# The second stage in two passes, with its weights prepared while the first stage still runs

## The chip, the cores and the metric

The kernel runs on one core of a Trainium2 chip. The metric is the device time of one execution in microseconds (us). The engines are TensorE (PE: matrix multiplies; PEld: its weight loads), VectorE (DVE), ScalarE (ACT), GpSimd (POOL) and SyncE (SP), which issues the DMAs. Each engine takes its instructions in a fixed order that is set when the kernel is built.

## The reference

Three blocks follow one another. The inputs are `q`, `k`, `v` of 8 batches, 8 heads, 576 positions and 64 columns, `phi` with 32 memory slots, and weights.

```python
# 1: attention over 32 memory slots, for each batch and head
a = softmax(phi, axis=positions)               # 576 x 32
k_m, v_m = a.T @ k, a.T @ v                    # 32 x 64
attn = softmax(q @ k_m.T / 8)                  # 576 x 32
x = attn @ v_m                                 # all heads side by side: 4608 x 512
# 2: gated layer, d_ff = 1536
x = (silu(x @ w_gate) * (x @ w_val)) @ w_out   # 4608 x 512
# 3: second layer, d_ff = 2048
h = x @ w_in
x = where(h > 0, h, exp(min(h, 0)) - 1) @ w_out2
```

The weights arrive as 64-bit floats, everything else in 32 bits.

## The kernel before

**Precision.** Each operand is split into a high part and a low part, and every product is made as three matmuls (high by high, low by high, high by low). A weight tile of 128 x 512 is loaded raw (64-bit, 512 KB) into a buffer `wr` and split by `split_w` (lines 71 to 85): two ScalarE copies (L77, L83), four VectorE instructions (L78, L79, L81, L82) that use a scratch tile `wc`, and two GpSimd instructions (L84, L85). L84 and L85 make the low part. `load_w` (L92) does this for one tile and takes two tiles from a pool, `whi` and `wlo`. There are 68 such loads: 24 of `w1g` (gate and value, in six pairs `p` of units with four pieces each), 12 of `w1o` (the output weight of each of 12 units) and 32 of `w2` (for the last block).

**Stage one** (the loop over batches `b`, L407) works on units 0 to 3 of the 12 units of the gated layer. `vw` (L112) multiplies the small matrix v_m by the gate and value weights of a pair, so that `gate1` and `val1` can multiply the attention weights `at` by the result directly. `down1` multiplies by the output weight and stores a partial sum to DRAM (`p1_d`, copied by L402). Beside it, a list `todo` of small tasks is worked off by `tick()`, a few after each unit: the back half of the attention of batch b+1 (q, scores, softmax, the transposed result `at`, stored at L340) and the front half of batch b+2 (phi, k, v; it ends in the store of `vt` at L280). All attention tiles lie in one pool, `at`. When batch 6 has been issued, this pool is closed, the pool `wb` of 32 weight tiles takes its room, and the loads of `w1g` pairs 2 to 4 and of four output weights are issued; the rest of the stage-two weights goes to pool `wa` (24 tiles), whose tiles held the weights of stage one.

**Stage two** (L512) goes once over all batches, two halves of 288 positions each. It reads `at` and `vt` back from DRAM, works on units 4 to 11, and sums their outputs in four PSUM accumulators `acc0` to `acc3`. `down2` lags two units behind. After unit 11, four VectorE additions (L486) add the partial sum, read from DRAM into the single buffer `p1`, and the result goes to `x1_d`. One unit is 12 matmuls for gate and value and 12 for the output, 288 columns wide; the `vw` of the next batch add 48 matmuls of 512 columns per batch.

**Stage three** (L594) takes nine blocks of 512 rows through 16 units with `w2`; all its matmuls are 512 columns wide. Twenty of the 32 loads of `w2` are written in stage two, twelve after it.

**Order.** The build places instructions by a simulated timeline. An instruction that comes later in the code may go ahead of others on its engine when its operands and its buffers are free.

Of the kernel before, what the change touches and what calls it, by code (L numbers as in the profile page):

```python
# [21 lines left out]
KD = DM // 128  # L22
# [7 lines left out]
NWB = 32  # L30
NWC = 8
# [3 lines left out]
def attention_moe_moe(ctx: ExitStack, tc: tile.TileContext, qT, phiT, kv, w1g, w1o, w2, out):  # L35
# [9 lines left out]
    wr_p = ctx.enter_context(tc.tile_pool(name="wr", bufs=2))  # L45
    wt_p = ctx.enter_context(tc.tile_pool(name="wt", bufs=1))
# [14 lines left out]
    ps_at = st_ps.enter_context(tc.tile_pool(name="ps_at", bufs=2, space=PSUM))  # L61
    st_at = ExitStack()
    at_p = st_at.enter_context(tc.tile_pool(name="at", bufs=1))
# [3 lines left out]
    p1_d = [dram.tile([128, KD, S], F32, name=f"p1d{b}") for b in range(B)]  # L67
    x1_d = [dram.tile([128, KD, S], F32, name=f"x1d{b}") for b in range(B)]


    def split_w(raw, hi, lo):
        lo32, hi32 = raw[:, :, 0], raw[:, :, 1]
        v = wt_p.tile([128, 512], F32, tag="wv", name="wv", bufs=2)
        c = wt_p.tile([128, 512], I32, tag="wc", name="wc")
        vi, cf = v.bitcast(I32), c.bitcast(F32)

        act(out=v, in_=hi32.bitcast(F32), func=AF.Copy, scale=2.0 ** -112)  # L77
        nc.vector.tensor_scalar(out=c, in0=vi, scalar1=3, scalar2=None, op0=ALU.logical_shift_left)  # L78
        stt(out=vi, in0=vi, scalar=-2 ** 31, in1=c, op0=ALU.bitwise_and, op1=ALU.bitwise_or)  # L79

        nc.vector.tensor_scalar(out=c, in0=vi, scalar1=-2 ** 23, scalar2=None, op0=ALU.bitwise_and)  # L81
        stt(out=cf, in0=lo32.bitcast(U32), scalar=2.0 ** -52, in1=cf, op0=ALU.mult, op1=ALU.mult)  # L82
        act(out=hi, in_=v, func=AF.Copy)  # L83
        nc.gpsimd.tensor_tensor(out=v, in0=v, in1=hi.bitcast(F32), op=ALU.subtract)  # L84
        nc.gpsimd.tensor_tensor(out=lo, in0=v, in1=cf, op=ALU.add)  # L85
# [77 lines left out]
    ident = at_p.tile([128, 128], F32, tag="ident", name="ident")  # L163
    make_identity(nc, ident)
    mask = at_p.tile([128, 4, 64], F32, tag="mask", name="mask")
# [14 lines left out]
    class Batch:  # L180
# [4 lines left out]
        def load_phi(self):  # L185
            self.ph = at_p.tile([128, 2, S], F32, tag="ph", name="ph")
            nc.sync.dma_start(out=self.ph, in_=phiT[self.b].rearrange("g p s -> p g s"))

        def load_kv(self, c):
            n = chunk(c)  # L190
            t = at_p.tile([128, 2, 512], F32, tag="kvr", name="kvr", bufs=2)
            nc.sync.dma_start(out=t[:n], in_=kv[self.b, 128 * c:128 * c + n])
            self.kvr[c] = t

        def load_q(self, c):
            n = chunk(c)
            t = at_p.tile([128, 512], F32, tag="qr", name="qr", bufs=2)
            nc.sync.dma_start(out=t[:, :4 * n], in_=qT[self.b, :, 512 * c:512 * c + 4 * n])
            self.qr[c] = t


        def phi(self):
            ph = self.ph
            nmx = at_p.tile([128, 2], F32, tag="nmx", name="nmx")
            nc.vector.tensor_reduce(out=nmx, in_=ph, op=ALU.max, axis=AX.X, negate=True)
            sm = at_p.tile([128, 2], F32, tag="sm", name="sm")
            for g in range(2):
                act(out=ph[:, g, :], in_=ph[:, g, :], func=AF.Exp, bias=nmx[:, g:g + 1],
                    accum_out=sm[:, g:g + 1])
            self.rs = at_p.tile([128, 2], F32, tag="rs", name="rs", bufs=2)  # L210
            nc.vector.tensor_scalar_add(out=self.rs, in0=sm, scalar1=1e-9)
            nc.vector.reciprocal(out=self.rs, in_=self.rs)

        def a_T(self, c0):
            if c0 == 0:
                self.ah = at_p.tile([128, NCH, 256], F32R, tag="ah", name="ah")
                self.al = at_p.tile([128, NCH, 256], F32R, tag="al", name="al")
# [12 lines left out]
        def kv_prep(self, c):  # L230
            n = chunk(c)
            t = self.kvr.pop(c)
            hi = at_p.tile([128, 2, 512], F32R, tag="kvh", name="kvh", bufs=2)
            lo = at_p.tile([128, 2, 512], F32R, tag="kvl", name="kvl", bufs=2)
            act(out=hi[:n], in_=t[:n], func=AF.Copy)
            lo_part(self.b and LO_KV[c], lo[:n], t[:n], hi[:n])
            self.kvs[c] = hi, lo
# [14 lines left out]
        def kv_out(self):  # L252
            self.kvm = at_p.tile([128, 2, 2, 256], F32, tag="kvm", name="kvm")
            mk = mask.rearrange("p h d -> p (h d)").unsqueeze(1).to_broadcast([128, 2, 256])
            for g in range(2):
                stt(out=self.kvm[:, g], in0=self.kvp[g], scalar=self.rs[:, g:g + 1], in1=mk,
                    op0=ALU.mult, op1=ALU.mult)

        def k_T(self):
# [4 lines left out]
            self.kT = at_p.tile([128, 2, 2, 128], F32R, tag="kT", name="kT")  # L264
# [17 lines left out]
        def q_prep(self, c):  # L282
            n = 4 * chunk(c)
            t = self.qr.pop(c)
            hi = at_p.tile([128, 512], F32R, tag="qh", name="qh", bufs=2)
            lo = at_p.tile([128, 512], F32R, tag="ql", name="ql", bufs=2)
# [4 lines left out]
        def score(self, c):  # L291
            n = chunk(c)
            if c == 0:
                self.sc = at_p.tile([128, NCH, 256], F32, tag="sc", name="sc")
# [6 lines left out]
            t = at_p.tile([128, 4, 64], F32, tag="sct", name="sct", bufs=2)  # L301
# [8 lines left out]
        def soft(self, c0, c1):  # L310
            n, k, sc = self.rows(c0, c1)
            mx = at_p.tile([128, 32, 1], F32, tag="mx", name="mx")[:n, :k]
# [4 lines left out]
        def soft2(self, c0, c1):  # L317
            n, k, sc = self.rows(c0, c1)
            sm = at_p.tile([128, 32, 1], F32, tag="smx", name="smx")[:n, :k]
# [85 lines left out]
    wl = []  # L405
    for b in range(B):
        todo = []  # L407
        bk = list(back_tasks(b + 1)) if b + 1 < B else []
        fr = list(front_tasks(b + 2)) if b + 2 < B else []
        for i in range(max(len(bk), len(fr))):  # L410
            todo += fr[i:i + 1] + bk[i:i + 1]
        if b + 1 < B:
            todo += vw_tasks(b + 1)
        done = [0, 0]

        def tick():
            done[0] += 1
            upto = min(len(todo), -(-len(todo) * (done[0] + 3) // 12))
# [17 lines left out]
        if b == B - 2:  # L436
            st_at.close()
            st_ps.close()
            wb_p = ctx.enter_context(tc.tile_pool(name="wb", bufs=NWB))
            for p in range(2, 5):  # L440
                for k in range(KD):
                    load_wg(p, k, wb_p)
                if p < 4:
                    for u in (2 * p, 2 * p + 1):
                        load_wo(u, wb_p)


    ps_acc = ctx.enter_context(tc.tile_pool(name="ps_acc", bufs=1, space=PSUM))
    ps_vw = ctx.enter_context(tc.tile_pool(name="ps_vw", bufs=1, space=PSUM))
    st_p1 = ExitStack()  # L450
    p1_p = st_p1.enter_context(tc.tile_pool(name="p1", bufs=1, side="right"))
    load_wo(8, wa_p)
    load_wo(9, wa_p)
    for k in range(KD):
        load_wg(5, k, wa_p)
    load_wo(10, wa_p)
    load_wo(11, wa_p)
# [3 lines left out]
    def more_w2(pool, n):  # L461
# [3 lines left out]
    at2, vt2 = {}, {}  # L465

    def load2(b):
        vt2[b] = av_p.tile([128, 2, KD, 128], F32R, tag="vt", name="vt2")
        nc.sync.dma_start(out=vt2[b].bitcast(F32), in_=vt_d[b].bitcast(F32))
        at2[b] = av_p.tile([128, 2, 2, S], F32R, tag="at", name="at2")  # L470
        nc.sync.dma_start(out=at2[b].bitcast(F32), in_=at_d[b].bitcast(F32))

    def load_p1(b, hf):
        t = p1_p.tile([128, KD, HS], F32, tag="p1", name="p1l")
        nc.sync.dma_start(out=t, in_=p1_d[b][:, :, HS * hf:HS * hf + HS])
        return t

    def down2(q):
        b, hf, u, hs, accs, p1 = q
        if u == UA:  # L480
            accs += [ps_acc.tile([128, HS], F32, tag=f"acc{m}", name=f"acc{m}") for m in range(KD)]
        for m in range(KD):
            down(accs[m], WO[u][0], hs, slice(128 * m, 128 * m + 128), u == UA, u == NU1 - 1)
        if u == NU1 - 1:
            for m in range(KD):
                tt(out=p1[:, m, :], in0=accs[m], in1=p1[:, m, :], op=ALU.add)  # L486
            nc.sync.dma_start(out=x1_d[b][:, :, HS * hf:HS * hf + HS], in_=p1)
# [17 lines left out]

    LAG = 2
    pend = []
    load2(0)
    for p in range(UA // 2, NU1 // 2):
        vw(0, p, vt2[0], ps_vw, "vw")  # L510
    vwq = []
    for b in range(B):  # L512
        for hf in range(2):
            p1 = load_p1(b, hf)
            accs = []
            if hf == 0 and b + 1 < B:
                load2(b + 1)
            for u in range(UA, NU1):
                s = gate1(b, u, at2[b], HS * hf)
                pend.append((b, hf, u, val1(b, u, at2[b], HS * hf, s), accs, p1))  # L520
                if len(pend) > LAG:
                    down2(pend.pop(0))
                if vwq:
                    q = vwq.pop(0)
                    vw(q[0], q[1], vt2[q[0]], ps_vw, "vw", (q[2],))
                    if q[0] == B - 1 and q[2] == 1:
                        more_w2(wb_p if q[1] < 5 else wa_p, 4)
                if hf == 1 and u % 2 == 1:
                    if b + 1 < B:
                        vwq += [(b + 1, u // 2, 0), (b + 1, u // 2, 1)]  # L530
                    elif u // 2 == 3:
                        nxt = load3(0)
                if b == 2 and hf == 0 and u % 2:
                    more_w2(wa_p, 1)
    for q in pend:
        down2(q)
    pend = []
    st_p1.close()
    st_r.close()
    more_w2(wb_p, 4)  # L540
    more_w2(wa_p, 4)
    wc_p = ctx.enter_context(tc.tile_pool(name="wc", bufs=NWC))
    more_w2(wc_p, 4)
# [93 lines left out]
```

## Time and profile before

| | |
|---|---|
| median of 3 runs | 1789.2 us (1788.12 to 1793.85) |
| the profiled execution | 1791.92 us, span 1790.1 us |
| mean granted TensorE clock | 0.971 of full speed |
| TensorE busy | 1708.9 us (95%) |
| VectorE busy | 1047.8 us (59%) |
| ScalarE busy | 770.8 us (43%) |
| GpSimd busy | 277.6 us (16%) |
| moved by DMA | 144.68 MB |

Busy times are sums over the whole span and hide the stages: stage one runs until some 470 us, stage two to 1000, stage three to the end. Matmuls overlap, so a busy TensorE is not one at its peak; counts of matmuls per us are a sharper measure. A row of the timeline names the line, the operation and, in brackets, how long the engine was idle before it and what ended the wait. In the stretches, PEclk is the granted clock as a share of full speed.

### The profile page before, as it was taken

The page shows a single profiled execution, that of the slowest core. Times are in us where ns is not written, and L with a number is a line of the kernel's source. Part 1 is how long each engine was busy: PE and PEld are TensorE (multiplying, and loading weights), DVE is VectorE, ACT ScalarE, POOL GpSimd, SP SyncE. Part 2 cuts the span into 40 slices and gives each one's busy share as a digit, 9 for nine tenths or more (in the row PEclk, how much of TensorE's full clock was granted, in tenths as well). Part 3 has the DMA queues.
Part 4 walks back from the last instruction along what each step waited for, and adds up shares of the span by engine and source line. Part 5 has one row for each costly group of instructions (what it writes and reads, how often), then busy time and mean ns, then how long its engine had stood idle before and what let it go on. Part 6 is the DMA issues. An engine that isn't in the chain of part 4 may idle for free.

```text
span 1790.1 us, 24102 instructions
## 1 busy us (share of the span) xinstructions
PE 1708.9 (95%) x9424; PEld 1496.5 (84%) x9424; DVE 1047.8 (59%) x1781; ACT 770.8 (43%) x1447; POOL 277.6 (16%) x197
## 2 busy tenths in 40 slices
PE   6689999999869999999999999999999999999998
PEld 4478998898759999999999878888888888888887
DVE  6887677657665333333368887455545555555554
ACT  5567666654433222322345444343434343434332
POOL 3552222114442000000034441000000000000000
PEclk8779999999969999999999999999999999999999
DMA  6555444234434121112225221010101010101000
GB/s 217 181 183 192 155 158 155 65 116 148 139 104 166 54 66 66 67 52 79 67 75 169 92 83 48 1 48 0 48 1 48 1 48 1 47 1 47 1 24 24
DMA packets 68209, 144.68 MB, mean 81 GB/s; under 512 B 7168, under 2 KB 38912, under 8 KB 66048
## 3 DMA queue, kind: packets, MB, share of 16 engines
q1 hardware_dynamic: 68096, 143.16, 24.1%
q8 instruction: 73, 1.20, 0.3%
q14 instruction: 40, 0.33, 0.1%
HBM read 101.19 MB, written 41.94 MB: 80 GB/s over the span
## 4 chain that ended last, share of the span: by engine, by line
PE 78%; DVE 9%; DMA 4%; ACT 3%; issue 2%; POOL 2%; SPq 0%; ACTq 0%; POOLq 0%; DVEq 0%
PE acc L581 7%; PE acc L582 7%; PE acc L583 7%; PE pu L557 7%; PE pu L555 6%; PE pu L556 6%; PE acc L139 3%; PE acc L138 3%; PE acc L137 3%; PE pg L132 2%; PE pv L132 2%; PE pg L133 2%; PE pg L134 2%; PE pv L134 2%; PE pv L133 2%
## 5 line engine op out<-in xcount | busy, mean ns | idle before, releaser
L581 PE MATMUL acc<-whi,hh 128*128 128x512 f32 x576 | 224.8, 390 | 3.3 <-ACT hh L143 3.3
L555 PE MATMUL pu<-x1s,whi 128*128 128x512 f32 x576 | 224.2, 389 | 1.6 <-DVE g L571 1.6
L582 PE MATMUL acc<-wlo,hh 128*128 128x512 f32 x576 | 224.2, 389 | 0.0
L557 PE MATMUL pu<-x1s,wlo 128*128 128x512 f32 x576 | 224.1, 389 | 0.0
L556 PE MATMUL pu<-x1s,whi 128*128 128x512 f32 x576 | 224.1, 389 | 0.0
L583 PE MATMUL acc<-whi,hl 128*128 128x512 f32 x576 | 223.0, 390 | 0.0
L570 DVE SCALAR_TENSOR_TENSOR g<-e,g 128x512 f32<-128x512 f32 x144 | 104.8, 727 | 157.1 <-ACT g L569 156.9
L84 POOL TENSOR_TENSOR wv<-wv,whi 128x512 f32<-128x512 f32 x68 | 102.1, 1501 | 587.3 <-ACT whi L83 469.6
L143 ACT ACTIVATE hh<-g 128x512 fp32r<-128x512 f32 x144 | 90.9, 632 | 217.0 <-DVE g L571 212.4
L159 DVE TENSOR_TENSOR h<-s,pv 128x288 f32<-128x288 f32 x192 | 86.5, 451 | 164.5 <-PE pv L134 135.3
L568 ACT ACTIVATE e<-g 128x512 f32<-128x512 f32 x144 | 90.8, 631 | 205.5 <-DVE g L567 205.2
L138 PE MATMUL acc<-hh,wlo 128*128 128x288 f32 x512 | 151.7, 298 | 2.7 <-POOL wlo L85 2.7
L145 DVE TENSOR_TENSOR hl<-g,hh 128x512 fp32r<-128x512 f32 x144 | 100.3, 697 | 87.0 <-ACT hh L143 87.0
L139 PE MATMUL acc<-hl,whi 128*128 128x288 f32 x512 | 149.7, 298 | 0.7 <-DVE hl L145 0.7
L137 PE MATMUL acc<-hh,whi 128*128 128x288 f32 x512 | 150.1, 296 | 0.3 <-ACT hh L143 0.3
L145 DVE TENSOR_TENSOR hl<-h,hh 128x288 fp32r<-128x288 f32 x192 | 108.4, 565 | 61.7 <-ACT hh L143 61.2
L143 ACT ACTIVATE hh<-h 128x288 fp32r<-128x288 f32 x192 | 85.0, 443 | 124.4 <-DVE h L159 123.9
L152 ACT ACTIVATE s<-pg 128x288 f32<-128x288 f32 x192 | 78.1, 408 | 123.6 <-PE pg L134 122.6
L581 PEld LDWEIGHTS acc<-whi,hh 128*128 128x128 f32 x576 | 108.1, 188 | 27.8 <-ACT hh L143 5.7
L567 DVE TENSOR_SCALAR g<-pu 128x512 f32<-128x512 f32 x144 | 99.3, 689 | 53.5 <-PE pu L557 53.3
L555 PEld LDWEIGHTS pu<-x1s,whi 128*128 128x128 f32 x576 | 108.1, 188 | 24.3 <-DVE g L571 2.0
L583 PEld LDWEIGHTS acc<-whi,hl 128*128 128x128 f32 x576 | 107.9, 187 | 24.5 <-DVE hl L145 2.2
(107 smaller groups left out, 4084.1 us busy)
## 6 DMA issues: line engine op xcount, KB each, us to landing
kvr<-kv SPq DMA_DIRECT2D x32, 512.0 KB, 3.9
wr<-w SPq DMA_DIRECT2D x32, 512.0 KB, 3.5
wr<-w1g SPq DMA_DIRECT2D x24, 512.0 KB, 3.6
atd<-at SPq DMA_DIRECT2D x8, 1152.0 KB, 4.9
p1d<-p SPq DMA_DIRECT2D x64, 144.0 KB, 2.0
p1l<-p1d SPq DMA_DIRECT2D x16, 576.0 KB, 4.1
at<-atd SPq DMA_DIRECT2D x8, 1152.0 KB, 5.2
x1d<-p1l SPq DMA_DIRECT2D x16, 576.0 KB, 3.3
```

The costliest lines, as they stand in the source:

```text
L137: mm(ps, lhsT=w[0][:, ms], rhs=hs[0], start=start, stop=False)
L138: mm(ps, lhsT=w[1][:, ms], rhs=hs[0], start=False, stop=False)
L139: mm(ps, lhsT=w[0][:, ms], rhs=hs[1], start=False, stop=stop)
L143: act(out=hh, in_=h, func=AF.Copy)
L145: tt(out=hl, in0=h, in1=hh.bitcast(F32), op=ALU.subtract)
L555: mm(ps, lhsT=wh[:, k, :], rhs=xh, start=k == 0, stop=False)
L556: mm(ps, lhsT=wh[:, k, :], rhs=xl, start=False, stop=False)
L557: mm(ps, lhsT=wl[:, k, :], rhs=xh, start=False, stop=k == KD - 1)
L570: stt(out=g, in0=e, scalar=1.0, in1=g, op0=ALU.add, op1=ALU.mult)
L581: mm(accs[c], lhsT=hs[0][:, cs], rhs=wh, start=u == 0, stop=False)
L582: mm(accs[c], lhsT=hs[0][:, cs], rhs=wl_, start=False, stop=False)
L583: mm(accs[c], lhsT=hs[1][:, cs], rhs=wh, start=False, stop=u == NU2 - 1)
```

## The change

- **Two passes.** Stage two goes over all batches twice: first with units 4 to 7 (weight pairs 2 and 3), then with units 8 to 11 (pairs 4 and 5). The first pass adds the partial sum of stage one and stores to a new DRAM buffer `p2_d`; the second adds that and stores to `x1_d`. Each pass reads `at` and `vt` of each batch.
- **Attention pool in two parts.** The front half (`fr`) is closed after batch 5, the back half (`bk`, on the right-hand side of the memory) after batch 7. From batch 6 on, a pool `wb` of 22 weight tiles takes the room of `fr`. The eight `w1g` loads of pairs 2 and 3 become tasks of batch 6; in batch 7 the tasks are the first `load2`, four output weights and the first two `vw` of stage two.
- **Spread.** In batches 6 and 7, the tasks are spread over 24 ticks instead of 12.
- **Later weights.** They are taken from a list `wq`, at most one per unit, each with the first pass index at which it may go: the second pass's `w1g` from index 0, its output weights from 2 (pool `wd`, 8 tiles), two `w2` from 4, ten from 9, two from 10, eight from 15. The last ten `w2` go to pool `wc` (20 tiles) after stage two.
- **Buffers.** Three raw buffers `wr` instead of two; two scratch tiles `wc` instead of one.

```diff
-NWB = 32
-NWC = 8
+NWB = 22
+NWD = 8
+NWC = 20
...
-    wr_p = ctx.enter_context(tc.tile_pool(name="wr", bufs=2))
-    wt_p = ctx.enter_context(tc.tile_pool(name="wt", bufs=1))
+    wr_p = ctx.enter_context(tc.tile_pool(name="wr", bufs=3))
+    wt_p = ctx.enter_context(tc.tile_pool(name="wt", bufs=2))
...
-    st_at = ExitStack()
-    at_p = st_at.enter_context(tc.tile_pool(name="at", bufs=1))
+    st_bk, st_fr = ExitStack(), ExitStack()
+    bk_p = st_bk.enter_context(tc.tile_pool(name="bk", bufs=1, side="right"))
+    fr_p = st_fr.enter_context(tc.tile_pool(name="fr", bufs=1))
...
+    p2_d = [dram.tile([128, KD, S], F32, name=f"p2d{b}") for b in range(B)]
...
-        v = wt_p.tile([128, 512], F32, tag="wv", name="wv", bufs=2)
+        v = wt_p.tile([128, 512], F32, tag="wv", name="wv")
...
+    SUB = ((2, 3), (4, 5))
...
+        if b == B - 2:
+            wb_p = ctx.enter_context(tc.tile_pool(name="wb", bufs=NWB))
+            ps_vw = ctx.enter_context(tc.tile_pool(name="ps_vw", bufs=1, space=PSUM))
+            fr += wg_tasks(2, wb_p)
+            fr += wg_tasks(3, wb_p)
+        if b == B - 1:
+            fr.append(lambda: load2(0))
+            fr += [lambda u=u: load_wo(u, wb_p) for u in (4, 5)]
+            fr += [lambda: vw2(0, 2), lambda: vw2(0, 3)]
+            fr += [lambda u=u: load_wo(u, wa_p) for u in (6, 7)]
...
+        spread = 12 if b < B - 2 else 24
 
         def tick():
             done[0] += 1
-            upto = min(len(todo), -(-len(todo) * (done[0] + 3) // 12))
+            upto = min(len(todo), -(-len(todo) * (done[0] + 3) // spread))
...
-        if b == B - 2:
-            st_at.close()
+        if b == B - 3:
+            st_fr.close()
             st_ps.close()
-            wb_p = ctx.enter_context(tc.tile_pool(name="wb", bufs=NWB))
-            for p in range(2, 5):
-                for k in range(KD):
-                    load_wg(p, k, wb_p)
-                if p < 4:
-                    for u in (2 * p, 2 * p + 1):
-                        load_wo(u, wb_p)
+    st_bk.close()
...
     def down2(q):
-        b, hf, u, hs, accs, p1 = q
-        if u == UA:
+        i, hf, u, hs, accs, p1 = q
+        u0, u1 = 2 * SUB[i // B][0], 2 * SUB[i // B][-1] + 1
+        if u == u0:
             accs += [ps_acc.tile([128, HS], F32, tag=f"acc{m}", name=f"acc{m}") for m in range(KD)]
         for m in range(KD):
-            down(accs[m], WO[u][0], hs, slice(128 * m, 128 * m + 128), u == UA, u == NU1 - 1)
-        if u == NU1 - 1:
+            down(accs[m], WO[u][0], hs, slice(128 * m, 128 * m + 128), u == u0, u == u1)
+        if u == u1:
             for m in range(KD):
                 tt(out=p1[:, m, :], in0=accs[m], in1=p1[:, m, :], op=ALU.add)
-            nc.sync.dma_start(out=x1_d[b][:, :, HS * hf:HS * hf + HS], in_=p1)
+            nc.sync.dma_start(out=(p2_d, x1_d)[i // B][i % B][:, :, HS * hf:HS * hf + HS], in_=p1)
...
+    wq = [(0, lambda p=p, k=k: load_wg(p, k, wa_p)) for p in SUB[1] for k in range(KD)]
+    wq += [(2, lambda u=u: load_wo(u, wd_p)) for u in range(8, 12)]
+    wq += [(4, lambda: more_w2(wa_p))] * 2
+    wq += [(B + 1, lambda: more_w2(wb_p))] * 10
+    wq += [(B + 2, lambda: more_w2(wa_p))] * 2
+    wq += [(2 * B - 1, lambda: more_w2(wa_p))] * 8
...
+    for i in range(2 * B):
+        b, us = i % B, range(2 * SUB[i // B][0], 2 * SUB[i // B][-1] + 2)
+        if i + 1 < 2 * B:
+            load2(i + 1)
+            vq = [(i + 1, p, g) for p in SUB[(i + 1) // B] for g in range(2)]
+        else:
+            vq = []
         for hf in range(2):
-            p1 = load_p1(b, hf)
+            p1 = load_p1(i, hf)
...
+                if wq and wq[0][0] <= i:
+                    wq.pop(0)[1]()
+                if vq and (hf or u >= us[2]):
+                    q = vq.pop(0)
+                    vw2(q[0], q[1], (q[2],))
...
+    wc_p = ctx.enter_context(tc.tile_pool(name="wc", bufs=NWC, side="right"))
+    more_w2(wc_p, len(todo2))
```

## Rows read from the trace of the kernel before

**Rows 1.** The page's part on engines: busy us (share), instructions.
```profile
PE 1708.9 (95%) x9424; PEld 1496.5 (84%) x9424; DVE 1047.8 (59%) x1781; ACT 770.8 (43%) x1447; POOL 277.6 (16%) x197
```

**Rows 2.** Stretches: us, then PE, PEld, DVE, ACT, POOL busy (instructions), PEclk, DMA share, GB/s.
```profile
25.00:75.00 50.00, 35.88 (x126) 23.48 (x126) 44.68 (x72) 27.25 (x52) 25.47 (x15) 0.67 0.49 157
...
356.00:400.00 44.00, 44.00 (x319) 42.16 (x318) 24.84 (x57) 23.88 (x56) 6.11 (x6) 1.00 0.32 119
400.00:475.00 75.00, 68.48 (x460) 63.84 (x459) 51.47 (x92) 36.26 (x83) 35.51 (x26) 1.00 0.47 156
475.00:525.00 50.00, 30.83 (x120) 23.24 (x119) 28.11 (x46) 14.73 (x28) 23.87 (x18) 0.67 0.31 103
525.00:560.00 35.00, 34.07 (x231) 32.33 (x230) 26.41 (x51) 15.72 (x34) 15.31 (x11) 0.98 0.38 125
560.00:900.00 340.00, 339.70 (x2363) 328.31 (x2364) 124.93 (x266) 101.62 (x220) 0.00 (x0) 1.00 0.22 72
900.00:1000.00 100.00, 99.57 (x690) 95.90 (x690) 75.34 (x139) 46.88 (x97) 43.15 (x30) 1.00 0.38 123
1000.00:1100.00 100.00, 95.11 (x406) 74.92 (x405) 85.69 (x128) 50.27 (x83) 37.95 (x26) 1.00 0.24 81
1100.00:1784.00 684.00, 684.00 (x3019) 566.25 (x3017) 369.98 (x545) 259.76 (x418) 0.00 (x0) 1.00 0.07 21
```

**Rows 3.** TensorE's timeline: start, us, engine, line, operation [idle before, what ended it].
```profile
484.72 0.50 PE L121 MATMUL pvw<-whi,vt 128*128 128x512 f32 x1 [1.85 <-ACT whi L83]
...
499.31 0.61 PE L138 MATMUL acc<-hh,wlo 128*128 128x288 f32 x1 [2.69 <-POOL wlo L85]
```

**Rows 4.** Timeline of VectorE (DVE), then of POOL, one weight at 499 us.
```profile
499.29 0.43 DVE L78 TENSOR_SCALAR wc<-wv 128x512 int32<-128x512 int32 x1 [2.49 <-POOL wlo L85]
499.75 0.69 DVE L79 SCALAR_TENSOR_TENSOR wv<-wv,wc 128x512 int32<-128x512 int32 x1
500.48 0.43 DVE L81 TENSOR_SCALAR wc<-wv 128x512 int32<-128x512 int32 x1
500.94 0.69 DVE L82 SCALAR_TENSOR_TENSOR wc<-wr,wc 128x512 f32<-128x512 uint32 x1
...
501.72 1.27 POOL L84 TENSOR_TENSOR wv<-wv,whi 128x512 f32<-128x512 f32 x1 [2.46 <-ACT whi L83]
503.07 1.26 POOL L85 TENSOR_TENSOR wlo<-wv,wc 128x512 fp32r<-128x512 f32 x1
```

**Rows 5.** Timelines of POOL and VectorE at 425; `hl` in 400–560 and in 560–900.
```profile
424.98 1.49 POOL L84 TENSOR_TENSOR wv<-wv,whi 128x512 f32<-128x512 f32 x1 [3.45 <-DVE wc L81]
...
425.24 1.78 DVE L82 SCALAR_TENSOR_TENSOR wc<-wr,wc 128x512 f32<-128x512 uint32 x1
...
L145 DVE TENSOR_TENSOR hl<-h,hh 128x288 fp32r<-128x288 f32 x30 | 21.9, 733 | 8.6 <-ACT hh L143 8.5
...
L145 DVE TENSOR_TENSOR hl<-h,hh 128x288 fp32r<-128x288 f32 x88 | 40.2, 457 | 35.9 <-ACT hh L143 35.8
```

**Rows 6.** Timeline of SyncE's queue, then of POOL.
```profile
356.63 0.32 SPq L280 DMA_DIRECT2D vtd<-vt  x1
...
525.27 10.69 SPq L94 DMA_DIRECT2D wr<-w  x3
...
393.72 1.29 POOL L84 TENSOR_TENSOR wv<-wv,whi 128x512 f32<-128x512 f32 x1 [27.11 <-DVE at L337]
```

**Rows 7.** Waits of SyncE's queue in 395–560; one VectorE line in 0–160.
```profile
SPq L94 <- DVE wc L82: 109.9, 22, 6.8
...
L78 DVE TENSOR_SCALAR wc<-wv 128x512 int32<-128x512 int32 x13 | 8.5, 655 | 2.7 <-POOL wlo L85 2.7
```

**Rows 8.** Timeline of SyncE's queue; one line of the page's DMA issues.
```profile
569.88 0.56 SPq L487 DMA_DIRECT2D x1d<-p1l  x1
573.24 0.54 SPq L475 DMA_DIRECT2D p1l<-p1d  x1
...
p1l<-p1d SPq DMA_DIRECT2D x16, 576.0 KB, 4.1
```

## What the change will do, predicted before it ran

> **What bounds the kernel now.** I read the page first. TensorE is busy 95% of the span [rows 1], so time can only be won where TensorE is not fed. The table of stretches comes next, because the share is a mean over stages, and the matmul counts in it say more than the busy column. From 560 to 900 us the second stage runs undisturbed: 2363 matmuls in 340 us, 6.95 per us, with 0.3 us idle [rows 2]. Against that rate the other stretches read:
>
> - 400–475: 460 matmuls are worth 66.2 us, so 8.8 us are lost while 13 weights are split (26 POOL instructions, two per weight).
> - 475–525: 120 matmuls are worth 17.3 us, so 32.7 us are lost; the granted clock averages 0.67 of 2.4 GHz, part of the work running at 1.2.
> - 525–560: 231 matmuls are worth 33.2 us; 1.8 us lost.
> - 900–1000: 690 are worth 99.3; 0.7 us lost, beside 15 weights.
> - 1000–1100 (third stage, all matmuls wide): the rate of 1100–1784 is 3019 in 684, 4.41 per us; 406 are worth 92.0, so 8.0 us are lost beside 13 weights.
>
> The 475–525 stretch has one wide matmul in six instead of one in nine, which makes its loss some 0.6 us smaller (estimate); I leave that aside. In 356–400 TensorE never idles.
>
> Next, the timeline of TensorE inside the 50 us. It stops first at 484.7 for a weight's high part and again and again for `whi` and `wlo` [rows 3]. The other engines' timeline then shows what one weight takes when nothing competes: four VectorE instructions, 0.43 + 0.69 + 0.43 + 0.69 us, then two of POOL (GpSimd), 1.27 + 1.26 us: 4.77 us, in series [rows 4]. Nine weights in 50 us are 5.6 us each [rows 2]. The reason that they come so late is the pool: the last front work of the attention stores its result at 356.6, yet POOL sits idle 27.1 us until the last attention tile is made, and starts on the 24 weights of stage two only at 393.7 [rows 6].
>
> **The change, part by part.**
>
> *Weights while the last two batches run.* The front half of the pool is given away at about 357 instead of 394, and the first pass needs 12 weights, not 24. At 5.6 us each they are done at 357 + 67 = 424, while TensorE before met no missing weight until 484.7. So the 32.7 us go: **−32.7**. The clock loss is inside this figure.
>
> *The stream of splits does not vanish, it moves.* A load starts as soon as its buffers are free, not where the code stands: raw tiles of `w2` that the code asks for in batch 2 of stage two are fetched at 525 [rows 6], some 55 us into a stage whose batch takes 16·3.86 = 62 us (below). So behind the 12 weights follow, without a pause, the 8 of units 8–11, their 4 output weights and 3 of `w2`: 27 in all, to about 357 + 27·5.6 = 508. What does one cost TensorE? Rows give 8.8/13 = 0.68 us (400–475) and 0.7/15 = 0.05 (900–1000). I take 0.68, since this stretch has the same neighbours (first-stage units and their copies). 27·0.68 = 18.4 against 10.6 lost before: **+7.8**. Bounds: 0.05 gives −9.2; the upper end is the rival below, 1.37 each, +26.4. Cover is thinnest in batch 6, where the last back half runs too: VectorE has 24.8 of 44 us taken there [rows 2], and 8 weights at 2.24 us add 18; if it overflows, units wait.
>
> *Later weights.* Twenty fall free late in pass one and after it (10 + 2) and late in pass two (8), beside stage-two units as at 900–1000: 20·0.05 = 1.0 against 0.7: **+0.3**. Ten, not 13, remain for the start of stage three: 10·0.62 = 6.2 against 8.0: **−1.8** (bounds −8.0, and +5.7 at 1.37 each).
>
> *Three raw buffers, second copy of `wc`.* SyncE waited 109.9 us in 22 waits for a raw buffer [rows 7], and the first VectorE instruction of a weight waited for the last POOL one of the weight before, which held the only `wc`. Both waits go. What is late next is the pair of engines itself: a VectorE instruction on two SBUF operands and a POOL instruction do not run together. At 425.24 the last VectorE step takes 1.78 us instead of 0.69, just until POOL's, begun at 424.98, is over [rows 5]. So the floor stays near 4.77 us and I change no pace. In the start-up, VectorE is busy 44.7 of 50 us in 25–75, and the `wc` wait idles it 2.7 us in all [rows 2, 7]: **−2.7**. Bounds: all idle of that stretch, −5.3; or 12 steps stretched from 0.69 to 1.78, +13.
>
> The Trainium skill, "SBUF — State Buffer", section "SBUF: two separate sides", states that VectorE and GpSimd share a port pair under an exclusive lock, for VectorE instructions with two SBUF inputs or in a two-port mode, and the loser waits for the whole instruction. This trace agrees (1.78 us for 0.69).
>
> *Two passes.* TensorE's matmuls are the same in number and shape. Added are 16 ends of an accumulation (64 VectorE additions of 0.45 us, 29 us over the 500 us of a stage in which VectorE is busy 37%), 16 stores and loads of partial sums and 8 more loads of both attention tiles (DMA share 0.22 in the quiet stage, at most doubled). The quiet stretch holds 11 such ends and idles 0.3 us: **+0.4** for 16. Cover: a store takes 573.24 − 569.88 = 3.4 us before the next load of the single `p1` buffer may go, that load 4.1 us [rows 8]: 7.5 us within a half-batch that now lasts 4·3.86 = 15.5 us. It fails if SyncE, whose waits for raw buffers last 5.0 us on average [rows 7], stands in front of both: then 2 us or so per half, and behind it wait the additions, the accumulators and the next `down2`. At ten halves +20, the upper end.
>
> *Spread 24 instead of 12.* The last batch's attention is issued by tick 18 of 25, not 9. Nothing waits for it as long as the rest of batch 6 (the last four output groups, 48 matmuls, 6.9 us) covers its tail; gone, a few us.
>
> **Sum.** −32.7 + 7.8 + 0.3 − 1.8 − 2.7 + 0.4 = −28.7. The profiled execution took 1791.9 us (span 1790.1), so 1763.2; it lies 2.7 above the median of the runs, from which it is 1760.5. I forecast **1762 us**.
>
> **Rivals.**
>
> 1. *The VectorE–POOL pair becomes the bound, and it gets slower.* With weights no longer separated by `wc`, they are ordered densely, one per unit. A unit of stage two is 340/88 = 3.86 us of TensorE [rows 2, 5]; the pair needs 4.77 + 0.46 (`hl`) = 5.23 us. If queues in fixed order tie units to weights, each weight costs 1.37 us. 57 weights lie behind the start-up: 57·1.37 = 78 us, against 52.0 lost before and 3 from the rest: 1789.2 + 24 = 1813. It decides from a price p of 0.95 (no change: 57p = 54.3); slower beyond 1.05. For it: `hl` already averages 733 ns instead of 457 beside splits [rows 5]. Against it: measured prices 0.05 to 0.68. By the exclusive lock of the page named above, this is the way it would go.
> 2. *Same pair, but only half felt:* p of 0.85 to 1.05 gives 1784 to 1794, no change to speak of. A milder form, 1.37 in the first 27 weights alone, gives 1762 + 18.6 = 1781.
> 3. *The gap only shrinks.* The 12 weights share batch 6 with the attention; if each takes over 8.6 us (103 us from 357 to about 460, my estimate of when pass one starts), TensorE still waits. At 10 us each, 17 us: 1779. For it: the start-up, where both run together and VectorE is full. Against it: the front half of the attention is over by then.
> 4. *Better:* the stream costs 0.05 a weight, as at 900–1000: 1762 − 7.8 − 9.2 = 1745; with nothing lost at the start of stage three either, 6.2 less: 1739.
>
> **How the numbers follow.** Forecast (1746 to 1778) 0.62; rival 1 0.11; rival 2 0.11, mild form 0.03 of these; rival 3 0.08; rival 4 0.08. Under 0.3% (5.4 us) this kernel's measurement cannot tell a change from none. Faster: 0.62 + 0.08 (rival 4) + 0.03 (the mild form) + 0.05 of rival 3 = 0.78. Same: 0.08 of rival 2 and 0.03 of rival 3 = 0.11. Slower: 0.11. The range goes from 1742 (the stream at its lower bound, 17.0 less, and the start-up at its own, 2.6 less) to 1793, nearly the end of rival 2; the slower case and what lies beyond 1742 are left out.
>
> **What would show it.** In the profile after: POOL's weight instructions begin near 357, not 394, in an unbroken stream to about 508; no stretch about 475–525 with a granted clock under 1.0 and none of TensorE's waits for `whi` or `wlo` after the start-up. The pace per weight stays at 5 us or more. Matmuls per us from 357 to 510 are 6.2 or so (0.68 lost per weight). Waits for `p1l` are absent. Wrong it would be if VectorE's `hl` and the last split step are stretched and TensorE waits for `h` or `hh` through each stream (rival 1), if the additions wait for a DMA (the two passes), or if the start-up moves by more than 5 us either way.

## The result, and the profile after

The changed kernel takes 1799.95 us (median of 5 runs, 1798.9 to 1800.95), 1.0055 times the kernel before, 95% interval [1.0041, 1.007]: slower by over 0.3%. The forecast was 1762 us with a range up to 1793. The profiled execution has a span of 1799.2 us, 9.1 more than before. The page's part on engines reads (against [rows 1]):

```profile
PE 1698.5 (94%) x9424; PEld 1491.3 (83%) x9424; DVE 1112.6 (62%) x1845; ACT 799.9 (44%) x1469; POOL 282.9 (16%) x197
```

VectorE gained 64 instructions (the 16 more ends) and 65 us, of which 64 additions of 0.45 us are only 29. ScalarE gained 22 instructions that no line of the diff asks for. Stretches of the kernel after, columns as in [rows 2], and two of the kernel before that were not shown:

```profile
0.00:175.00 175.00, 126.10 (x662) 102.07 (x663) 146.60 (x234) 107.41 (x198) 73.70 (x55) 0.84 0.58 190
175.00:375.00 200.00, 186.88 (x1231) 170.15 (x1230) 119.86 (x233) 139.27 (x258) 43.23 (x27) 0.97 0.38 128
375.00:475.00 100.00, 85.72 (x529) 79.06 (x528) 92.33 (x147) 60.02 (x121) 56.02 (x39) 0.91 0.49 169
475.00:550.00 75.00, 67.14 (x450) 62.84 (x449) 58.06 (x92) 30.52 (x68) 27.07 (x19) 0.98 0.48 167
550.00:690.00 140.00, 140.00 (x980) 135.59 (x979) 57.11 (x126) 42.03 (x91) 0.00 (x0) 1.00 0.41 138
690.00:760.00 70.00, 66.02 (x452) 62.46 (x451) 56.68 (x95) 28.36 (x61) 28.73 (x20) 1.00 0.52 177
...
930.00:1000.00 70.00, 66.67 (x465) 63.45 (x464) 56.13 (x100) 29.69 (x64) 22.46 (x16) 1.00 0.52 166
1000.00:1110.00 110.00, 106.52 (x477) 86.02 (x476) 81.98 (x120) 50.30 (x82) 28.56 (x20) 1.00 0.17 56
```

```profile
0.00:175.00 175.00, 133.67 (x631) 106.10 (x632) 139.88 (x229) 104.94 (x194) 75.43 (x56) 0.80 0.59 197
175.00:375.00 200.00, 198.24 (x1336) 181.40 (x1335) 132.53 (x260) 127.47 (x263) 43.74 (x29) 1.00 0.39 129
```

The gap near 500 is gone: after 175 us no stretch above falls under a granted clock of 0.91 (its lowest part, 400 to 425, has 0.77; the start-up, 25 to 75, has 0.60, before 0.67). In its place small losses stand wherever weights are split, and one stands where hardly any are: from 175 to 375 us the kernel after does 105 matmuls fewer.

To compare kernels I count the time lost in a stretch: its length less its matmuls at the spacing that they have undisturbed, 0.227 us for 512 columns and 0.1335 for 288 (the quiet stretches), and about 0.1 for the few narrower ones (estimate). Full-rate work comes to some 1640 us in every kernel here, so differences of lost time add up to the differences of the spans. "First stream" is 375 to 550.

| lost, us | 0–175 | 175–375 | 375–475 | 475–550 | 550–690 | 690–760 | 930–1000 | 1000–1110 |
|---|---|---|---|---|---|---|---|---|
| before (span 1790.1) | 82.0 | 8.8 | 10.0 | 33.2 | 1.5 | 0 | 0.4 | 8.2 |
| after (1799.2) | 75.1 | 25.0 | 25.3 | 11.8 | 0 | 5.4 | 4.6 | 6.2 |
| after less before | −6.9 | +16.2 | +15.3 | −21.4 | −1.5 | +5.4 | +4.2 | −2.0 |

**175 to 375: activation tables.** ScalarE's timeline of the kernel after around 260 us, then the two rows of TensorE's that answer to it:

```profile
256.40 1.28 ACT L156 ACT_TABLE_LOAD   x1
257.70 0.41 ACT L156 ACTIVATE s<-pg 128x288 f32<-128x288 f32 x1
258.13 1.28 ACT L319 ACT_TABLE_LOAD   x1
...
261.90 1.28 ACT L156 ACT_TABLE_LOAD   x1
...
263.62 1.28 ACT L319 ACT_TABLE_LOAD   x1
...
265.35 1.28 ACT L156 ACT_TABLE_LOAD   x1
266.64 0.41 ACT L156 ACTIVATE s<-pg 128x288 f32<-128x288 f32 x1
```

```profile
263.65 0.40 PE L136 MATMUL pv<-at,vw 128*128 128x288 f32 x1 [1.67 <-ACT s L156]
...
267.11 0.61 PE L136 MATMUL pg<-at,vw 128*128 128x288 f32 x1 [2.40 <-ACT s L156]
```

Silu (L156) and the softmax's exp (L319) take turns, and each turn loads another table for 1.28 us. The same two waits, 1.67 and 2.40 us, come again at 318 and 322, one batch later. The groups of table loads for silu, before and after:

```profile
L152 ACT ACT_TABLE_LOAD x12 | 15.4, 1283 | 0.2
```

```profile
L156 ACT ACT_TABLE_LOAD x23 | 29.5, 1283 | 0.4
```

Over all lines there are 25 loads before and 47 after, which are the 22 instructions: 28 us more of ScalarE. Not one of them is written in either kernel: the order built for ScalarE decides how often silu and exp alternate. The Trainium skill, "ScalarE: Activation LUTs", section "What ACT_TABLE_LOAD costs", has the load as an instruction of ScalarE of some 1283 ns, and adds some 1380 ns of drain for every switch. The trace agrees on the load (1283 ns) and shows no drain of that length: at 256.40 + 1.28 the load is over, and the next instruction begins at 257.70. The section "Rules for kernel authors" of that page of the Trainium skill says to do all of one set before switching; what it costs here not to is measured below (e3 and e10).

**The streams: the pair.** VectorE's instructions of a split and `hl`, kernel after, 400 to 500 us (group, count, busy us, mean ns, idle before):

```profile
L86 DVE SCALAR_TENSOR_TENSOR wc<-wr,wc 128x512 f32<-128x512 uint32 x16 | 15.4, 960 | 0.2
L149 DVE TENSOR_TENSOR hl<-h,hh 128x288 fp32r<-128x288 f32 x19 | 14.1, 743 | 3.3 <-ACT hh L147 3.3
L83 DVE SCALAR_TENSOR_TENSOR wv<-wv,wc 128x512 int32<-128x512 int32 x15 | 13.3, 890 | 0.1
L82 DVE TENSOR_SCALAR wc<-wv 128x512 int32<-128x512 int32 x15 | 11.1, 739 | 0.8 <-ACT wv L81 0.8
L85 DVE TENSOR_SCALAR wc<-wv 128x512 int32<-128x512 int32 x16 | 9.0, 564 | 0.1
```

The four split instructions average 739, 890, 564 and 960 ns, where they took 430, 690, 430 and 690 undisturbed [rows 4]: 0.91 us more for each weight. VectorE's timeline in that stream, then POOL's:

```profile
440.47 1.32 DVE L149 TENSOR_TENSOR hl<-h,hh 128x288 fp32r<-128x288 f32 x1 [0.24 <-ACT hh L147]
441.71 1.76 DVE L86 SCALAR_TENSOR_TENSOR wc<-wr,wc 128x512 f32<-128x512 uint32 x1
443.40 1.27 DVE L129 TENSOR_TENSOR vw<-pvw,vw 128x512 fp32r<-128x512 f32 x2
444.60 0.41 DVE L82 TENSOR_SCALAR wc<-wv 128x512 int32<-128x512 int32 x1
445.05 1.67 DVE L83 SCALAR_TENSOR_TENSOR wv<-wv,wc 128x512 int32<-128x512 int32 x1
```

```profile
440.19 1.29 POOL L88 TENSOR_TENSOR wv<-wv,whi 128x512 f32<-128x512 f32 x1 [4.86 <-ACT whi L87]
441.56 1.37 POOL L89 TENSOR_TENSOR wlo<-wv,wc 128x512 fp32r<-128x512 f32 x1
442.89 1.72 POOL L88 TENSOR_TENSOR wv<-wv,whi 128x512 f32<-128x512 f32 x1
444.69 1.47 POOL L89 TENSOR_TENSOR wlo<-wv,wc 128x512 fp32r<-128x512 f32 x1
```

Read the ends: `hl` ends at 441.79, just after POOL's first; L86 ends at 443.47, after POOL's second (442.93); L83, begun at 445.05, ends at 446.72, after POOL's that was begun at 444.69 and over at 446.16. Each of the three takes over twice its own time, and ends 0.3 to 0.6 us after the POOL instruction that it met. TensorE's longest waits in the same stream:

```profile
400.05 0.61 PE L141 MATMUL pd<-hh,whi 128*128 128x288 f32 x1 [2.33 <-DVE h L163]
...
421.11 0.61 PE L136 MATMUL pg<-at,vw 128*128 128x288 f32 x1 [3.43 <-ACT s L156]
...
444.13 0.50 PE L125 MATMUL pvw<-whi,vt 128*128 128x512 f32 x1 [1.61 <-DVE vw L129]
...
466.77 0.50 PE L125 MATMUL pvw<-whi,vt 128*128 128x512 f32 x1 [1.80 <-DVE vw L129]
```

At 444.13 TensorE wants a `pvw` buffer, which VectorE empties (L129, at 443.40) only after the stretched L86. It no longer waits for weights; it waits for VectorE's and ScalarE's ordinary work, which stands behind the split's. The longest wait, 3.43 us, is of the other kind: a table load for the softmax's exp and one back for silu stand just before that silu, in ScalarE's timeline:

```profile
417.06 1.28 ACT L319 ACT_TABLE_LOAD   x1
...
419.35 1.28 ACT L156 ACT_TABLE_LOAD   x1
```

TensorE's waits in this stream come to 22.0 us; the rest of the loss is matmuls wider apart than undisturbed, at a granted clock of 0.91 in 375 to 475. 27 weights end in 375 to 550, and 37.1 us are lost: 1.37 us each, the figure of rival 1 (how far that is luck, see below). The 29 later ones cost 5.4 + 4.6 + 6.2 = 16.2 us, 0.56 each.

### The profile page after: what moved, and what is told of

The parts are those of the page before. It is cut to its first block, busy times and chain, and to the rows that moved or that the text cites. A ratio compares the mean times of both kernels' runs of the same rounds, so it can differ in the third digit from the quotient of the medians.

```text
span 1799.2 us, 24284 instructions
## 1 busy us (share of the span) xinstructions
PE 1698.5 (94%) x9424; PEld 1491.3 (83%) x9424; DVE 1112.6 (62%) x1845; ACT 799.9 (44%) x1469; POOL 282.9 (16%) x197
## 4 chain that ended last, share of the span: by engine, by line
PE 76%; DVE 15%; ACT 4%; issue 4%; DMA 2%; POOL 0%; DVEq 0%; ACTq 0%; SPq 0%; POOLq 0%
PE acc L599 7%; PE acc L600 7%; PE acc L601 7%; PE pu L573 7%; PE pu L574 7%; PE pu L575 7%; PE acc L141 3%; PE acc L143 3%; PE acc L142 3%; DVE wc L82 3%; DVE wv L83 2%; PE pg L136 2%; PE pv L136 2%; PE pg L137 2%; PE pv L138 2%
## 5 line engine op out<-in xcount | busy, mean ns | idle before, releaser
L88 POOL TENSOR_TENSOR wv<-wv,whi 128x512 f32<-128x512 f32 x68 | 104.5, 1537 | 532.8 <-ACT whi L87 423.2
L149 DVE TENSOR_TENSOR hl<-g,hh 128x512 fp32r<-128x512 f32 x144 | 104.4, 725 | 90.5 <-ACT hh L147 90.5
L136 PE MATMUL pg<-at,vw 128*128 128x288 f32 x384 | 119.0, 310 | 15.8 <-ACT s L156 8.2
L156 ACT ACTIVATE s<-pg 128x288 f32<-128x288 f32 x192 | 78.3, 408 | 117.9 <-PE pg L138 115.8
L573 PEld LDWEIGHTS pu<-x1s,whi 128*128 128x128 f32 x576 | 108.2, 188 | 24.9 <-DVE g L589 2.5
```

The costliest lines, as they stand in the source:

```text
L136: mm(ps, lhsT=wh, rhs=ah, start=g == 0, stop=False)
L149: tt(out=hl, in0=h, in1=hh.bitcast(F32), op=ALU.subtract)
L573: mm(ps, lhsT=wh[:, k, :], rhs=xh, start=k == 0, stop=False)
```

## The experiments

Two theories stood after the result. **Buffers:** the second scratch tile `wc` lets VectorE begin the next weight while POOL still works on the last, so the two block one another and the splits come denser; the rest of the change does what was forecast. **Passes:** the early weights and the two passes themselves cost the time, whatever the buffers. The table loads were a third suspect.

### Buffers or passes: e1 and e2

e1 is the kernel after with the old buffer counts; the diff is against after. e2 is the kernel before with the new counts alone: the same two edits the other way.

```diff
-    wr_p = ctx.enter_context(tc.tile_pool(name="wr", bufs=3))
+    wr_p = ctx.enter_context(tc.tile_pool(name="wr", bufs=2))
...
-        c = wt_p.tile([128, 512], I32, tag="wc", name="wc")
+        c = wt_p.tile([128, 512], I32, tag="wc", name="wc", bufs=1)
```

> The changed kernel with two raw buffers and one scratch tile, as before the change; two passes, split pool and spread stay. Theory A (the buffers did it: they pack the splits densely and bring 22 more table loads to ScalarE): 25 table loads again, the 16.5 us lost in 175-375 come back, the start-up gives its 7 us back, the splits between 375 and 550 cost 0.7 us each instead of 1.3 (18 us less) and those near 700 and 960 next to nothing (10 us less): about 1764 us. Theory B (two passes, with their extra ends, stores and reads, did it): still 1795 or more.

> The kernel before with three raw buffers and two scratch tiles, nothing else. Theory A: the start-up gains 7 us, stage one loses 15 us to table loads (some 45 of them instead of 25), the gap near 500 shortens as weights come every 4.8 us instead of 5.6 (24 of them: up to 19 us), but the splits near 950 and 1050 cost 1 us each (15 to 20 us): 1790 to 1805 us. Theory B: the buffers are innocent and shorten the gap: 1770 us or less.

e1: 1761.4 us (1759.5 to 1766.1), 0.9829 of before [0.9809, 0.9849]. e2: 1822.6 us (1821.2 to 1823.8), 1.0166 [1.0149, 1.0184]. The kernel before, timed anew beside each group of runs, took 1789.2 us beside the kernel after, 1792.7 beside e1 to e4, 1789.9 beside e5 to e8 and 1788.9 beside e9 to e12, so a difference between two groups is uncertain by some 4 us. The new counts cost 38.6 us on the changed kernel (1799.95 − 1761.4; 42.0 when each is taken against the kernel before beside it) and some 30 on the old one, and the passes with their early weights gain about what was forecast for them. e2 lies above what either theory allowed: the gap that I expected to shorten does not (375 to 550 loses 43.5 us, 43.2 before), and 930 to 1000 loses 19.5 us instead of 0.4. In e1 the first stream loses 19.0 us, in which 25 weights end, and POOL starts its first one at 356.86 (in the kernel after only at 381.26):

```profile
356.86 1.30 POOL L88 TENSOR_TENSOR wv<-wv,whi 128x512 f32<-128x512 f32 x1 [13.52 <-ACT whi L87]
```

The late start goes with the table loads: the first weight is at 370.0 us in e9 (43 loads), at 379.0 in e6 (47) and, with the kernel after's own buffer counts, at 350.9 in e11 (3). What exactly holds it up was not followed.

### Which of the two buffers: e5, e6 and e9

e5 takes only the second scratch tile back, e6 only the third raw buffer (each one of e1's two edits). e9 is e5's kernel again, timed with an interval.

> The changed kernel with three raw buffers but one scratch tile. If the scratch tile is what kept the splits apart (the first VectorE step of a weight waits for the last GpSimd one of the weight before), only the table loads stay (43 in the order as built, against 47 and 25): the price per weight between 375 and 550 is near 0.7 us, and the time near 1761 + 15 = 1776 us. If the raw buffers kept them apart, 1795 us or more.

> The changed kernel with two raw buffers but two scratch tiles. If the scratch tile is the spacer, nearly all of the harm is here: 47 table loads, 1.2 us or more per weight, 1793 to 1802 us. If the raw buffers were the spacer, some 1776 us.

> The kernel after with one scratch tile `wc` and three raw buffers, now with an interval, because one run of it gave 1755.8 us, 5 less than the version with both old buffer counts (1761.4). Theory (the second scratch tile is what costs, the third raw buffer saves some of the start-up): 1752 to 1760 us, ratio to before 0.979 to 0.983. If the 5 us were chance: 1761.

e5: 1755.8 us; e9: 1755.6 us (1754.7 to 1757.6), 0.9812 of before [0.9794, 0.983]. e6: 1789.5 us, one run. Both came out below my figures (1776 for e5, of which I had put 15 on the table loads; 1793 to 1802 for e6). e9's median is 5.8 us below e1's, but the ratios' intervals overlap ([0.9794, 0.983] and [0.9809, 0.9849]), so a gain by the third raw buffer alone is not shown. The second scratch tile alone loses some 28 on e1, and 44.3 on e9 when it is added to three raw buffers. VectorE's groups in e9, 400 to 500 us, are to be held against those of the kernel after above:

```profile
L149 DVE TENSOR_TENSOR hl<-h,hh 128x288 fp32r<-128x288 f32 x24 | 18.5, 771 | 5.2 <-ACT hh L147 5.2
L86 DVE SCALAR_TENSOR_TENSOR wc<-wr,wc 128x512 f32<-128x512 uint32 x17 | 13.6, 799 | 0.3
L83 DVE SCALAR_TENSOR_TENSOR wv<-wv,wc 128x512 int32<-128x512 int32 x17 | 11.7, 686 | 0.2
...
L85 DVE TENSOR_SCALAR wc<-wv 128x512 int32<-128x512 int32 x17 | 7.2, 422 | 0.3
L82 DVE TENSOR_SCALAR wc<-wv 128x512 int32<-128x512 int32 x16 | 6.8, 424 | 10.6 <-POOL wlo L89 10.6
```

With one scratch tile L82 waits for POOL's last step, 10.6 us in this stretch. That wait keeps L82, L83 and L85 clear of POOL: they take their own 424, 686 and 422 ns. Only L86 and `hl` still meet it. The stretches of e9, beside those of the kernel after above:

```profile
375.00:475.00 100.00, 91.28 (x596) 85.88 (x595) 73.25 (x137) 60.39 (x123) 47.38 (x33) 0.95 0.48 163
475.00:550.00 75.00, 75.00 (x536) 73.19 (x535) 57.88 (x112) 34.52 (x74) 32.74 (x22) 1.00 0.60 201
```

VectorE is busy 73 of 100 us instead of 92, and TensorE does 596 and 536 matmuls instead of 529 and 450. From e9 to the kernel after the spans differ by 46.3 us (1752.9 to 1799.2), and the lost times by 5.2 in 0–175, 5.5 in 175–375, 9.7 and 12.0 in the first stream, 5.6 in 690–760, 4.8 in 930–1000 and 3.2 in 1000–1110, together 46.0.

### The pair taken apart: e4, e7 and e12

e4 leaves out POOL's first instruction (L88), the first line of the diff. e7 gives both of POOL's to VectorE, as the diff shows, in the kernel after, and e12 does the same in e9's kernel.

```diff
-        nc.gpsimd.tensor_tensor(out=v, in0=v, in1=hi.bitcast(F32), op=ALU.subtract)
-        nc.gpsimd.tensor_tensor(out=lo, in0=v, in1=cf, op=ALU.add)
+        tt(out=v, in0=v, in1=hi.bitcast(F32), op=ALU.subtract)
+        tt(out=lo, in0=v, in1=cf, op=ALU.add)
```

> The changed kernel without the subtraction v - hi (first of the two GpSimd instructions of a split), so the low parts hold other numbers; VectorE's work is the same. Theory of the shared pair: it is held 3.5 us per weight instead of 4.8, VectorE's split instructions are stretched less, a weight between 425 and 475 takes VectorE 2.6 us instead of 3.5, and the 54 us lost beside splits fall by some 30: 1765 to 1775 us. If VectorE's own work is what is too much, or the order, the time stays within 6 us of 1800.

> The changed kernel with both GpSimd instructions of a split on VectorE: no contention over the pair there, but 1.38 us more of VectorE's own work per weight (3.6 us instead of 2.24). Theory: in the dense bursts the stretched instructions already cost VectorE 3.5 us per weight, so handing the work over changes little: 1790 to 1805 us, with VectorE's mean times at their minimum (hl 0.46 us). If the pair's blocking reaches TensorE by more than VectorE's time, it is faster by 15 us or more.

> Three raw buffers, one scratch tile, and both POOL instructions of a split on VectorE. Theory A (blocking inside the pair costs more than VectorE's own time for the two instructions; with two scratch tiles the move took the time from 1800 to 1764): 1742 to 1754 us. Theory B (with one scratch tile the pair hardly blocks, and VectorE, now with some 1.4 us more per weight, holds up the units of stage one): 1758 to 1770 us.

e4: 1753.9 us, one run, below the 1765 to 1775 that I expected: half of POOL's work gone takes 46 us away, as much as the scratch tile brought. It also makes each weight's chain shorter by that instruction, so it does not tell blocking from length. e7: 1763.6 us, one run, well below what I expected. e12: 1747.7 us (1746.6 to 1748.4), 0.9764 of before [0.9745, 0.9784], as theory A said. Two of VectorE's groups in e12, 400 to 500 us:

```profile
L83 DVE SCALAR_TENSOR_TENSOR wv<-wv,wc 128x512 int32<-128x512 int32 x17 | 11.7, 688 | 0.3
...
L149 DVE TENSOR_TENSOR hl<-h,hh 128x288 fp32r<-128x288 f32 x25 | 11.2, 451 | 0.1
```

`hl` is back at 451 ns, and the low part costs VectorE 2 × 0.686 us per weight. By that the move adds 1.37 us of VectorE per weight, more than the 0.91 by which blocking stretches the split; I had expected little from it for this reason. What I left out is `hl`, stretched by 0.3 us on average (743 ns against 451), and that POOL is stretched too (L88 and L89 take 1485 and 1441 ns in 400 to 500 of the kernel after, 1.27 and 1.26 us undisturbed [rows 4]): a weight's six steps add up to 6.1 us on the two engines there and to 3.6 us on VectorE alone in e12.

Without POOL the second scratch tile still costs 16 us (e7 against e12), against 44.3 with it (after against e9). So some 28 of the 44 us come with the pair (e7 is one run). The rest comes without POOL, with denser splits and another order, which no run tells apart: e7's first 100 us of the stream lose 16.5 us, e12's 6.5, and e7 has 47 table loads, e12 31, with 25.2 and 18.4 us lost in 175 to 375.

### The tables: e3, e8, e10 and e11

e3 puts Tanh in Silu's place throughout (first diff, against after); there is then one table load in all. The other three keep the function (second diff): in stage one alone, silu is made as x(1 + tanh(x/2)), and the half goes into the copy of the partial sum. That leaves 3 loads and costs VectorE one instruction more per unit and half. e8 is that on e1, e10 on e9's kernel, e11 on the kernel after.

```diff
-        act(out=s, in_=pg, func=AF.Silu)
+        act(out=s, in_=pg, func=AF.Tanh)
```

```diff
-        act(out=s, in_=pg, func=AF.Silu)
+        if u < UA:
+            act(out=s, in_=pg, func=AF.Tanh, scale=0.5)
+            stt(out=s, in0=s, scalar=1.0, in1=pg, op0=ALU.add, op1=ALU.mult)
+        else:
+            act(out=s, in_=pg, func=AF.Silu)
...
-        act(out=io, in_=ps, func=AF.Copy)
+        act(out=io, in_=ps, func=AF.Copy, scale=0.5)
```

> The changed kernel with tanh in place of silu (the gate's function is another, the instructions are as many): exponential and tanh need no table load between them. Table theory: the loss in 175-375 falls from 25 us to that of before, 9, and some 6 more come back where batch 7's softmax ran, 1775 to 1780 us. If the table loads are only a mark of another order and cost TensorE nothing, the loss in 175-375 stays at 20 us or more and the time at 1795 to 1800.

> Two passes with two raw buffers and one scratch tile, and in stage one silu made as x(1 + tanh(x/2)), the half put into the copy of the partial sum: the table loads go from 25 to 3, for 64 more VectorE instructions of 0.45 us. By the price of the 22 added loads (16 to 20 us, or 0.8 us each) the 22 that remain would be worth up to 10 us in the start-up and stage one: 1750 to 1757 us. If loads in a better order hide behind other waits, no gain, and VectorE's added 29 us may cost: 1760 to 1770 us.

> Three raw buffers, one scratch tile, and silu in stage one made as x(1 + tanh(x/2)) with the half in the copy of the partial sum, so that ScalarE needs no second table there; VectorE has one more instruction per unit and half. Theory A (the 43 table loads of this version stand in TensorE's way in 175 to 375 us, where it loses 19.1 us; the same change took the version with 25 loads from 11.3 to 14.8 us lost there, VectorE's extra work): lost there about 14 to 15, time 1748 to 1753 us. Theory B (the loads are hidden, or VectorE's added work costs as much): 1755 to 1760 us.

> The kernel after, with three raw buffers and two scratch tiles, and the same silu of stage one without a second table. It tells how much of the 38 us between after (1800) and the old buffers (1761) are table loads and how much is the pair VectorE-POOL. Theory A (mostly the pair: 57 weights at about 0.9 us): 1785 to 1797 us, with 375 to 550 us still losing over 30 us. Theory B (the table loads, or the order that they make, are the larger part): 1765 to 1780 us.

e3: 1775.2 us, one run, 25 below the kernel after; lost in 175–375: 7.0 us instead of 25.0. The table loads (and the order that goes with them) are thus worth some 18 us there when nothing is paid for their absence. e8: 1758.5 us (1755.1 to 1761.2), 0.9824 of before [0.9798, 0.985], beside e1's [0.9809, 0.9849]: the intervals overlap, so no gain is shown where only 22 loads go (25 to 3). e10: 1749.0 us (1748.3 to 1749.5), 0.9773 [0.9757, 0.9789], 6.7 below e9, timed beside it, as theory A said. e11: 1792.6 us, one run, 7 below the kernel after, also as theory A said.

Two scratch tiles against one, with and without the loads, and with the split on VectorE (e11 and e7 are one run each):

| us | one scratch tile | two | difference |
|---|---|---|---|
| silu and exp alternate | 1755.6 (e9, 43 loads) | 1799.95 (after, 47) | 44.3 |
| one table in stage one | 1749.0 (e10, 3) | 1792.6 (e11, 3) | 43.6 |
| split wholly on VectorE | 1747.7 (e12, 31) | 1763.6 (e7, 47) | 15.9 |

The table loads are a cost, but the scratch tile's is the same without them (first two rows). Only the split's move to VectorE takes most of it away.

**Versions that beat both kernels.** e1, e8, e9, e10 and e12 are faster than before and after, and e5 and e7 are by one run each (e3 and e4 compute something else). The fastest, e12 at 0.9764 and e10 at 0.9773, are not told apart by their intervals. The two edits together were not tried.

## Why the prediction was wrong

The step that failed is "Three raw buffers, second copy of `wc`": I put it at −2.7 us ("so the floor stays near 4.77 us and I change no pace"), with a bound of +13. It measured +38.6 to +42.0, and the second scratch tile by itself +44.3 (e9 to after): it took away the wait that kept three of VectorE's split instructions clear of POOL, and the price of the weights behind the start-up rose with it. The rest, e1, lies 31.3 us under the kernel before beside it (25.8 between the profiled spans); its terms add up to a forecast of −26.0.

- **Weights while the last two batches run, −32.7, and the stream, +7.8: right in size.** In e1 the first stream loses 19.0 us, before 43.2: −24.2, forecast −24.9 (175 to 375, where its first two weights end, loses 2.5 more than before). A weight costs there 19.0/25 = 0.76 us, near the 0.68 taken. After 175 us TensorE waits for no `whi` or `wlo`, neither in e1 nor in the kernel after. POOL starts at 356.9, forecast 357, but the pace is 6.6 us a weight and not 5.6: twelve are done at 440 and 27 at 531, forecast 424 and 508. In the kernel after the price is 1.37, and the start 381.3.
- **Later weights, +0.3 and −1.8.** In e1 +0.6 in 930–1000 and +1.6 in 690–760; the start of stage three −4.8. In the kernel after +5.4, +4.2 and −2.0: the same step paid again for the buffers. Errors of 2 to 3 us in these terms and in the stream's cancel in e1's sum.
- **The buffers, −2.7: wrong.** The half that I meant, the start-up, has the right sign and went past its bound of −5.3: 82.0 us lost before, 82.3 in e1, 69.9 with three raw buffers (e9), some 74 with two scratch tiles (e6), 75.1 with both. So one more buffer of either kind gives 8 to 12 there, and both together no more than one. What I missed is that the wait for the only `wc` did work: it kept three of the four VectorE instructions of a split from meeting POOL. I had the price of a meeting (1.78 us for 0.69, [rows 5]; not "just until POOL's is over": that instruction ends at 427.02, POOL's at 426.47) and the exclusive lock of the Trainium skill's page "SBUF — State Buffer", section "SBUF: two separate sides", and used both for a floor on the pace instead of asking how often VectorE would now meet POOL. My upper bound of 13 counted 12 weights of the start-up, though 56 follow it.
- **No row bore on the table loads,** and no step speaks of them. They were 25 before, with hardly any wait in 175–375. Either buffer raises them (e9 43, e6 47; e1 25), and 175 to 375 loses 11.3 us in e1, 19.5 in e9, 25.0 after, but 14.8, 15.1 and 17.1 in the same three with one table in stage one (e8, e10, e11). So of the raw buffer's 12 us in the start-up the times show 5.8 at most.
- **Two passes, +0.4: right.** 550 to 690 loses nothing. TensorE's waits for `p1l`, forecast absent, come to 0.2 us in e1 and to 2.0 in the kernel after.
- **Spread, 0:** not tried by itself; it is in e1's 1761.4.

Rival 1, at 0.11, came nearest: the pair does get slower and holds TensorE up. Its price of 1.37 us is met in the first 27 weights, but partly by luck: it was worked out for a pair that sets a pace of 5.23 us, while the weights there come every 5.9 us, the longest wait is for table loads, and some 16 of the scratch tile's 44 us stay when POOL has no part in the split. The other 29 weights cost 0.56 each (56 follow the start-up, not the 57 of the prediction). That is 53.3 us in all or 0.95 each, the price at which rival 1 saw no change; the time lies 9 above that because of 175 to 375, where the table loads stand (+16.2, in no step of mine), less the start-up (−6.9). The chance was too low: against it stood prices measured with one scratch tile, and the change took that very condition away.

## What to carry to other kernels

Before a buffer is added to take a wait away, ask what the wait keeps apart: here the single scratch tile kept VectorE and GpSimd from working on two weights at once, and a second one cost 44 us (28 of them gone when VectorE did all of the split). A price per item read from a trace holds only under the waits of that trace. After any change that lets an order be rebuilt, count the table loads on ScalarE; they stand in no line of the code.

## What had not been expected of the hardware

- Two GpSimd instructions of 1.27 us were dearer to this kernel than the same two on VectorE, where they take 0.686 us: 8 us with one scratch tile (e9 to e12), 36 with two (after to e7).
- A one-operand VectorE instruction (L82, 128x512) is stretched in the streams too: 739 ns on average in 400–500 and 959 in 690–760 of the kernel after, against 424 in e9.
- A table load lasts 1283 ns every time, and one or two of them between two units hold TensorE up by 1.67 and 2.40 us.
